# Retention and a hard-swish MLP on one core: the first pieces' Q loads issued later, two copies moved to VectorE, the last stores spread over three queues

## The chip, the cores and the metric

The kernel runs on one core of a Trainium2 chip. A core has TensorE (matmuls, PE in the profile, its weight loads PEld), VectorE (DVE), ScalarE (ACT), GpSimd (POOL) and SyncE (SP), each working through its own instructions in order, and 16 DMA engines that all queues share. The metric is the device time of one execution in microseconds (us), the median of repeated runs.

## The reference, cut to what matters

Inputs are q, k, v of shape (8, 8, 576, 64): batch, heads, sequence, head size. Weights are w_in (512 x 2048) and w_out (2048 x 512). All are float32.

```python
scores = (1/8) * q @ k.T                    # per batch and head, 576 x 576
gamma = 1 - 2 ** (-5 - head)
ret = scores * (gamma ** (i - j) if i >= j else 0)
x = (ret @ v)                               # heads side by side: 4608 tokens x 512
h = x @ w_in
g = h * clip(h + 3, 0, 6) / 6
out = g @ w_out                             # 4608 x 512
```

## The kernel before

The sequence of each batch is cut into pieces of 128 positions (four per batch), plus one of 64 that is paired with another batch's. Retention runs piece by piece: scores within the piece, masked; outputs from the masked scores and V; and a state that carries K and V of the earlier pieces on to the next. The decay is split into a factor on Q, a factor on V and a constant per piece on the state. Outputs are written as float16, transposed, into `xt`; every 512 tokens of `xt` go through the first GEMM with w_in (`g1`, line 577), the activation on ScalarE and VectorE (lines 585, 586), and the second GEMM with w_out (`g2`, line 635, or in seven products instead of eight, `g2_seven`, line 720). The retention of later pieces is woven in between the GEMMs. The order of instructions on each engine is the order in which the program writes them.

The change lies at both ends.

*The head.* Pieces 0 to 3 (`EARLY = 4`) come before the first GEMM and are built without transposing DMAs. `load_kv(c)` loads K and V by GpSimd's queue (line 103; the transfer converts them to float16). `load_q(c)` loads Q as float32 by SP's queue (line 120) into `qf`; with a second argument the load waits until that instruction has ended. `cast_q` makes it float16 on ScalarE (line 128). `q_by_pe` multiplies Q by a diagonal matrix `dq` on TensorE, which transposes and scales it (line 265), and copies the result to `qk[:, 0]` on ScalarE (line 272; for piece 3 in two halves, line 270). `k_by_pe` transposes K on TensorE (line 256) and copies it to `qk[:, 1]` on ScalarE (line 257). `scale_v` applies V's factor on VectorE (line 245). `scores` multiplies K by Q (line 343) and masks on VectorE (line 347), `inter` and `intra` make a piece's output from the state and the masked scores (lines 361, 372) and copy it to `xt` (line 377). `state_early` updates the state (lines 314, 318) and multiplies it by `gfull` on VectorE (line 323). Piece 3 has its own `scores_last` (line 283, masks in two halves on VectorE, line 286) and `out_last` (lines 297, 303, copies to `xt` line 306), after which the first GEMM starts. `fill_gfull` writes the decay constants of the state into `gfull`. `warm(n, cols)` runs n matmuls on zeros. GpSimd issues, in this order, K and V of pieces 0 to 3, then w_in in five parts (line 131), then w_out and the pieces from 4 on.

`newest[0]` holds the TensorE instruction that a later load is told to wait for. Before the change, Q 0 and Q 1 are loaded at once, Q 2 after the matmuls of `q_by_pe(0)` and Q 3 after the transposes of `k_by_pe(0)`.

*The tail.* In the last call of `g2_seven` each quarter of the output goes out by `store_quarter`: half of its rows by SP's queue and half by ScalarE's (line 688). The last product of the seven leaves two halves `xo` and `xtu` in PSUM; `copy_half(u)` copies each to SBUF on ScalarE (line 751), and `store` sends it out by SP's and ScalarE's queues (line 625).

Of the kernel before, what the change touches and what calls it, by code (L numbers as in the profile page):

```python
# [13 lines left out]
ALU = mybir.AluOpType  # L14
# [3 lines left out]
def kernel(  # L18
# [16 lines left out]
    nc = tc.nc  # L35
# [89 lines left out]
                reason="the first pieces have the queues")  # L125

    def cast_q(c):
        nc.scalar.copy(loaded[c]["q16"], plain_q[c])

    def load_win(f0, f1):  # L130
        return nc.gpsimd.dma_start(
# [11 lines left out]
    nc.gpsimd.iota(wide, pattern=[[1, P + 1]], base=-1, channel_multiplier=-1,  # L143
                   allow_small_or_imprecise_dtypes=True)
    load_q(0)
    load_q(1)
    load_kv(0)
    zeros = const.tile([P, MBLK], FP16)
    nc.vector.memset(zeros, 0.0)
# [6 lines left out]
    for h in range(H):  # L156
# [15 lines left out]
    nc.vector.tensor_tensor(out=ident16, in0=mask01, in1=mask_wide[:, 0:P], op=ALU.subtract)  # L172

    dq = const.tile([P, H, P], FP16)
    nc.vector.tensor_tensor(out=dq, in0=ident16[:, None, :].to_broadcast([P, H, P]),
                            in1=gq[:, :, None].to_broadcast([P, H, P]), op=ALU.mult)
    gqv = const.tile([P, 2, H, D], FP16)
    cast_q(0)
    nc.scalar.copy(gqv[:, 1], gv[:, :, None].to_broadcast([P, H, D]))
# [10 lines left out]
    nc.vector.memset(gfull, 0.0)  # L190

    def fill_gfull():
        nc.scalar.copy(gfull[0:HALF, :, 0:D],
                       gc[0:HALF, 0, :, None].to_broadcast([HALF, NPAIR, D]))
        nc.scalar.copy(gfull[HALF:P, :, D:2 * D],
                       gc[HALF:P, 0, :, None].to_broadcast([HALF, NPAIR, D]))

    def fill_gq():
        nc.scalar.copy(gqv[:, 0], gq[:, :, None].to_broadcast([P, H, D]))
# [52 lines left out]
    def k_by_pe(c, tag=None):  # L252
        kn = loaded[c]["kn"]
        pk = bank_or(tag, [P, NPAIR, P], FP16, name=f"trk_{c}")
        for p in range(NPAIR):
            newest[0] = nc.tensor.transpose(pk[:, p, :], kn[:, 2 * p:2 * p + 2, :], ident16)
        nc.scalar.copy(qk_of(c)[:, 1], pk)

    def q_by_pe(c):
        q16, qk = loaded[c]["q16"], qk_of(c)  # L260
        pq = bank([P, NPAIR, P], FP32, name=f"trq_{c}")
        for p in range(NPAIR):
            for h2 in range(2):
                r = slice(h2 * HALF, h2 * HALF + HALF)
                newest[0] = nc.tensor.matmul(
                    pq[r, p, :], q16[:, 2 * p + h2, :], dq[:, 2 * p + h2, :],
                    start=(p == 0), stop=(p == NPAIR - 1), skip_group_check=True)
        if c == EARLY - 1:
            for p in (0, 2):
                nc.scalar.copy(qk[:, 0, p:p + 2], pq[:, p:p + 2])  # L270
        else:
            nc.scalar.copy(qk[:, 0], pq)

    def scores_last(c):

# [60 lines left out]
    def scores(c, late=9):  # L336
        run_later(late)
        qk = st[c]["qk"]
        sc = psum.tile([P, 2, NPAIR, P], FP32, tag="sc", name=f"sc_{c}")
        for p in range(NPAIR):  # L340
            for h2 in range(2):
                r = slice(h2 * HALF, h2 * HALF + HALF)
                nc.tensor.matmul(sc[:, h2, p, :], qk[r, 1, p, :], qk[r, 0, p, :],
                                 start=True, stop=True)
        at = work.tile([P, 2, NPAIR, P], FP16, tag="at", bufs=3, name=f"at_{c}")
        st[c]["at"] = at
        later.append(lambda: nc.vector.tensor_tensor(
            out=at.rearrange("t a b s -> t (a b) s"), in0=sc.rearrange("t a b s -> t (a b) s"),
            in1=mask_b, op=ALU.mult))
# [328 lines left out]
    def store_quarter(kb, i, j, src):  # L678

        cols = slice(NH * j, NH * j + NH)  # L680
        if kb < B:
            r0 = kb * S + TH * i
            nc.sync.dma_start(out[r0:r0 + TH, cols].rearrange("(u p) n -> p u n", u=2), src)
        else:
            rest = out.rearrange("(m x s) n -> x s m n", x=2, s=S)
            for x in range(2):
                queue = nc.scalar if x else nc.sync
                queue.dma_start(rest[x, MAIN:S, 2 * i:2 * i + 2, cols],
                                src[x * HALF:x * HALF + HALF])

    def g2_seven(kb, last=False):

        gt = gts[kb]

        def w(i, j):
            return wout16[:, KH * i:KH * i + KH, NH * j:NH * j + NH]

        def a(i, j):
            return gt[:, KH * j:KH * j + KH, TH * i:TH * i + TH]

        def s(name):
            return sums[kb, name]

        acc = {}

        def get(name):
            if name not in acc:
                if last and name == "x":
                    acc[name] = [psum.tile([P, NH], FP32, tag=t, name=f"x{t}_{kb}")
                                 for t in ("o", "tu")]  # L710
                else:
                    whole = bank([P, 2, NH], FP32, name=f"{name}_{kb}")
                    acc[name] = [whole[:, 0], whole[:, 1]]
                    wholes[name] = whole
            return acc[name]

        def product(name, u, left, right, first):
            dst = get(name)[u]
            for c in range(KH):
                newest[0] = nc.tensor.matmul(  # L720
                    dst, left()[:, c, P * u:P * u + P], right[:, c, :],
                    start=(first and c == 0 and (u == 0 or name not in wholes)),
                    stop=(c == KH - 1), skip_group_check=True)

        kept, wholes = {}, {}

        def parts(name, tile):
            if name in wholes:
                return [(wholes[name], tile)]
            return [(acc[name][u], tile[:, u]) for u in range(2)]  # L730

        def keep(name):
            kept[name] = work.tile([P, 2, NH], FP32, tag="keep_" + {"m5": "m1"}.get(name, name), bufs=1,
                                   name=f"keep_{name}_{kb}")
            for src, dst in parts({"m5": "z"}.get(name, "x"), kept[name]):
                nc.scalar.copy(dst, src)

        def total(i, j, name, src):
            osb = work.tile([P, 2, NH], FP32, tag="osb", bufs=4, name=f"osb_{kb}_{i}_{j}")
            for (a0, dst), (_, a1) in zip(parts(src, osb), parts(src, kept[name])):  # L740
                nc.vector.tensor_tensor(out=dst, in0=a0, in1=a1, op=ALU.add)
            store_quarter(kb, i, j, osb)

        def copy_total():
            osb = work.tile([P, 2, NH], FP32, tag="osb", bufs=4, name=f"osb_{kb}_1_0")
            nc.scalar.copy(osb, wholes["x"])
            store_quarter(kb, 1, 0, osb)

        def copy_half(u):
            osb = work.tile([P, NH], FP32, tag="osb", bufs=4, name=f"osh_{kb}_{u}")  # L750
            nc.scalar.copy(osb, acc["x"][u])
            store(kb, 2 + u, slice(0, NH), osb)

        def unit(name, u, left, right, first, then=()):
            def do():
                product(name, u, left, right, first)
                for f in then:
                    f()
            return do

        plan = [
            ("x", lambda: a(0, 0), w(0, 0), True, [lambda: keep("m1")]),
            ("y", lambda: a(0, 1), w(1, 0), True,
             [lambda: total(0, 0, "m1", "y"), lambda: token_sums(kb, "s3")]),
            ("x", lambda: s("s2"), wts["t2"], False, [lambda: keep("u2")]),
            ("z", lambda: s("s1"), wts["t1"], True,
             [lambda: keep("m5"), lambda: token_sums(kb, "s4")]),
            ("x", lambda: s("s3"), wts["t3"], False, [lambda: total(1, 1, "m5", "x")]),
            ("z", lambda: s("s4"), w(1, 1), False, [lambda: total(0, 1, "u2", "z")]),
            ("x", lambda: a(1, 1), wts["t4"], False, [] if last else [copy_total]),  # L770
        ]
        units = []
        for n, (name, left, right, first, then) in enumerate(plan):
            for u in range(2):
                after = then if u else []
                if last and n == len(plan) - 1:
                    after = [lambda u=u: copy_half(u)]
                units.append(unit(name, u, left, right, first, after))
        return units
# [10 lines left out]
    for i in range(4):  # L790
        if i == 2:
            load(4)
        load_wout(4 * i, 4 * i + 4)

    scale_v(0)
    q_by_pe(0)
    load_q(2, newest[0])
    warm(2, MBLK)
    cast_q(1)
    k_by_pe(0)  # L800
    load_q(3, newest[0])
    fill_gfull()
    for c in range(EARLY):
        if c:
            inter(c - 1)
            intra(c - 1)
        if c < EARLY - 1:
            scores(c)
            run_later(9)
            if c:  # L810
                k_by_pe(c + 1)
            state_early(c)
            run_later(9)
            if not c:
                k_by_pe(c + 1)
            q_by_pe(c + 1)
            if c + 2 < EARLY:
                cast_q(c + 2)
            scale_v(c + 1)
        else:  # L820
            scores_last(c)
# [280 lines left out]
```

## Time and profile before

| what | value |
|---|---|
| median of 3 runs | 294.07 us (294.04 to 294.34) |
| the profiled execution's own time | 294.43 us |
| span of its instructions | 292.6 us |
| TensorE busy | 281.1 us, 96% |
| VectorE, ScalarE, GpSimd busy | 227.6, 169.1, 104.3 us |
| granted TensorE clock | 1.0 |
| start of the first GEMM (L577) | 18.17 us |
| first and second copy of the last halves (L751) | 287.45 and 288.49 us |

The profile's times run from the start of the span, so the execution's own time is 1.8 us more. Times of steps below come from this one execution; the median of the runs is 0.36 us under it.

### The profile page before, as it was taken

Reading aid. Unit: us, or ns where it says so; the run is one execution under the profiler, and the core shown is the slowest. Engines: PE = TensorE matmul, PEld = TensorE weight load, DVE = VectorE, ACT = ScalarE, POOL = GpSimd, SP = SyncE. Lnnn points to the kernel's source line nnn. Section 1 sums busy time; section 2 is a strip of 40 time slices with the busy share of each in tenths; the row PEclk is TensorE's granted clock in tenths of the full one; section 3 lists DMA queues with packets and bytes.
Section 4 is the critical chain, followed back from the end, with each engine's and each line's share of the span. In section 5 each row is a group of like instructions: output and inputs, shape, how many; then the busy total and the mean of one; then the engine's idle time right before and its main releaser. Section 6 shows DMA issues by size and latency. Waiting matters only on the chain.

```text
span 292.6 us, 8351 instructions
## 1 busy us (share of the span) xinstructions
PE 281.1 (96%) x3492; PEld 174.7 (60%) x3492; DVE 227.6 (78%) x377; ACT 169.1 (58%) x301; POOL 104.3 (36%) x130
## 2 busy tenths in 40 slices
PE   7699999999989999999999999999999999999993
PEld 2454445544544587458745874587458745874682
DVE  4858656798758997899789988998899588728860
ACT  6668537784357744774486448644864286338711
POOL 8753578159523432443234324455550000000000
PEclk9999999999999999999999999999999999999999
DMA  9999999999999989997999799979992240120014
GB/s 137 177 205 203 191 157 215 165 126 137 132 215 166 160 85 120 168 141 81 121 163 143 77 127 170 136 82 123 160 139 47 74 110 0 38 81 30 0 39 109
DMA packets 156631, 36.21 MB, mean 124 GB/s; under 512 B 143792, under 2 KB 155568, under 8 KB 156592
## 3 DMA queue, kind: packets, MB, share of 16 engines
q0 software_dynamic: 113104, 17.83, 89.3%
q1 hardware_dynamic: 42896, 17.31, 30.5%
q8 instruction: 27, 0.44, 0.7%
q10 hardware_dynamic: 592, 0.52, 0.5%
q14 instruction: 12, 0.10, 0.1%
HBM read 36.70 MB, written 9.44 MB: 158 GB/s over the span
## 4 chain that ended last, share of the span: by engine, by line
PE 91%; DMA 4%; POOL 2%; DVE 1%; issue 1%; ACT 0%; ACTq 0%; POOLq 0%
PE ph L577 41%; PE x L720 14%; PE pout L635 9%; PE z L720 8%; PE y L720 5%; DMA kn<-in_k_dram 3%; PE o L483 3%; PE sc L450 2%; PE o L504 1%; PE u L535 1%; PE ph L600 1%; POOL kn L103 1%; DMA out_dram<-osb 1%; PE xtu L720 1%; PE xo L720 1%
## 5 line engine op out<-in xcount | busy, mean ns | idle before, releaser
L577 PE MATMUL ph<-xt,win 128*128 128x512 f16 x560 | 122.3, 379 | 0.0
L586 DVE SCALAR_TENSOR_TENSOR gt<-u,ph 128x512 f16<-128x512 f32 x144 | 95.7, 685 | 22.6 <-ACT u L585 21.4
L585 ACT ACTIVATE u<-ph,cb 128x512 f32<-128x512 f32 x144 | 98.4, 688 | 25.7 <-PE ph L577 25.1
L577 PEld LDWEIGHTS <-win 128*128 128x128 f16 x560 | 54.7, 98 | 64.4
L103 POOL DMA_DIRECT2D kn<-in_k_dram x40 | 34.0, 850 | 40.7 <-PE ph L577 15.4
L103 POOL DMA_DIRECT2D qv<-in_v_dram x40 | 33.8, 846 | 38.8 <-PE ph L577 16.2
L720 PEld LDWEIGHTS <-sum_s 128*128 128x128 f16 x448 | 42.7, 98 | 5.3
L103 POOL DMA_DIRECT2D qv<-in_q_dram x36 | 30.2, 839 | 28.7 <-PE z L720 10.4
L720 PEld LDWEIGHTS <-gt 128*128 128x128 f16 x336 | 32.1, 98 | 5.5
L635 PE MATMUL pout<-wout,gt 128*128 128x512 f16 x128 | 29.6, 379 | 0.1
L720 PE MATMUL x<-wsum_t,sum_s 128*128 128x256 f16 x192 | 22.9, 273 | 0.0
L556 ACT CAST tm<-th 128x256 f16<-128x256 f32 x24 | 9.7, 405 | 20.3 <-DVE th L551 20.1
L635 PEld LDWEIGHTS <-gt 128*128 128x128 f16 x128 | 11.9, 98 | 13.2 <-issue 0.4
L456 DVE TENSOR_TENSOR at<-sc,mask 128x1024 f16<-128x1024 f32 x14 | 17.0, 1217 | 1.9 <-PE sc L450 1.9
L676 DVE TENSOR_TENSOR sum_s<-gt 128x1024 f16<-128x1024 f16 (+1 forms) x21 | 18.1, 864 | 0.2
L332 DVE TENSOR_TENSOR qv<-qv,gqv 128x1024 f16<-128x1024 f16 x26 | 17.8, 684 | 0.0
L514 ACT CAST xt<-o 128x512 f16<-128x512 f32 x28 | 15.0, 585 | 4.6 <-PE o L504 4.6
L567 DVE TENSOR_TENSOR ta<-u,th 128x256 f32<-128x256 f32 x24 | 10.2, 424 | 6.3 <-ACT th L554 5.2
L720 PE MATMUL z<-wout,sum_s 128*128 128x256 f16 x112 | 14.5, 274 | 0.0
L720 PE MATMUL y<-wout,gt 128*128 128x256 f16 x112 | 14.3, 273 | 0.0
L720 PE MATMUL z<-wsum_t,sum_s 128*128 128x256 f16 x112 | 13.6, 273 | 0.0
L720 PE MATMUL x<-wout,gt 128*128 128x256 f16 x96 | 11.5, 272 | 0.0
(118 smaller groups left out, 255.3 us busy)
## 6 DMA issues: line engine op xcount, KB each, us to landing
out_dram<-osb SPq DMA_DIRECT2D x32, 256.0 KB, 3.2
kn<-in_k_dram POOLq DMA_DIRECT2D x32, 128.0 KB, 5.9
qv<-in_v_dram POOLq DMA_DIRECT2D x32, 128.0 KB, 6.0
qv<-in_q_dram POOLq DMA_DIRECT2D x28, 128.0 KB, 5.9
wout<-in_moe_w_out_dram POOLq DMA_DIRECT2D x4, 512.0 KB, 15.2
win<-in_moe_w_in_dram POOLq DMA_DIRECT2D x3, 512.0 KB, 12.3
qf<-in_q_dram SPq DMA_DIRECT2D x4, 256.0 KB, 4.6
win<-in_moe_w_in_dram POOLq DMA_DIRECT2D x2, 256.0 KB, 8.3
```

Source lines behind the costliest of these rows:

```text
L103: loaded[c]["dma"].append(nc.gpsimd.dma_start(dst[p0:p0 + n], src[b, :, s0:s0 + n, :].rearrange("h s d -> s h d")))
L332: scaled = nc.vector.tensor_tensor(out=qv, in0=qv, in1=gqv, op=ALU.mult)
L456: nc.vector.tensor_tensor(out=at.rearrange("t a j p s -> t (a j p) s"), in0=sc.rearrange("t a j p s -> t (a j p) s"), in1=mask64[:, None, ...
L514: nc.scalar.copy(xt_at(cs[0], 0, 2 * P).rearrange("e p (j x s) -> e p j x s", j=2, x=2) [:, :, :, half, :], o[half].rearrange("e j p s -> ...
L556: nc.scalar.copy(tm, ta)
L567: nc.vector.tensor_tensor(out=ta, in0=st[c]["u"][1], in1=st[c]["sum"], op=ALU.add)
L577: newest[0] = nc.tensor.matmul(ph, win16[:, dmc, P * fc:P * fc + P], xt_of(kb)[:, dmc, :], start=(dmc == 0), stop=(dmc == NCC - 1))
L585: nc.scalar.activation(u, ph, ACTF.Relu, bias=cb[:, 0:1], scale=1.0 / 6.0)
L586: nc.vector.scalar_tensor_tensor(out=gts[kb][:, fc, :], in0=u, scalar=1.0, in1=ph, op0=ALU.min, op1=ALU.mult)
L635: nc.tensor.matmul(pout, gt[:, fc, P * mc:P * mc + P], wout16[:, fc, :], start=(fc == 0), stop=(fc == NFC - 1))
L676: nc.vector.tensor_tensor(out=s(which)[:, c0:c1], in0=x(), in1=y(), op=op)
L720: newest[0] = nc.tensor.matmul(dst, left()[:, c, P * u:P * u + P], right[:, c, :], start=(first and c == 0 and (u == 0 or name not in whol ...
```

## The change

Loads: Q 1 is no longer loaded at once but after `dq` has been computed on VectorE. Q 2 is loaded after the scores matmuls of piece 0 and Q 3 after the transposes of K 1; for that, `newest[0]` is now set in `scores` and no longer in `q_by_pe`.

Order in the loop over the first pieces: the cast of Q c+1 stands after `state_early(c)`, and with it come K and Q of piece c+1, K first for pieces 1 and 2, Q first for piece 3. For piece 3, K instead of Q is copied to `qk` in two halves. One more matmul of 512 columns on zeros follows `k_by_pe(0)`.

`fill_gfull` is done by VectorE instead of ScalarE, ahead of `scale_v(0)`.

Tail: of the quarter (0, 1) the second half of the rows is stored by GpSimd's queue instead of ScalarE's, and the second of the last two halves is copied by VectorE instead of ScalarE.

```diff
     def cast_q(c):
-        nc.scalar.copy(loaded[c]["q16"], plain_q[c])
+        return nc.scalar.copy(loaded[c]["q16"], plain_q[c])
...
     load_q(0)
-    load_q(1)
     load_kv(0)
...
-    nc.vector.tensor_tensor(out=dq, in0=ident16[:, None, :].to_broadcast([P, H, P]),
-                            in1=gq[:, :, None].to_broadcast([P, H, P]), op=ALU.mult)
+    load_q(1, nc.vector.tensor_tensor(
+        out=dq, in0=ident16[:, None, :].to_broadcast([P, H, P]),
+        in1=gq[:, :, None].to_broadcast([P, H, P]), op=ALU.mult))
...
     def fill_gfull():
-        nc.scalar.copy(gfull[0:HALF, :, 0:D],
-                       gc[0:HALF, 0, :, None].to_broadcast([HALF, NPAIR, D]))
-        nc.scalar.copy(gfull[HALF:P, :, D:2 * D],
-                       gc[HALF:P, 0, :, None].to_broadcast([HALF, NPAIR, D]))
+        nc.vector.tensor_copy(gfull[0:HALF, :, 0:D],
+                              gc[0:HALF, 0, :, None].to_broadcast([HALF, NPAIR, D]))
+        nc.vector.tensor_copy(gfull[HALF:P, :, D:2 * D],
+                              gc[HALF:P, 0, :, None].to_broadcast([HALF, NPAIR, D]))
...
     def k_by_pe(c, tag=None):
...
-        nc.scalar.copy(qk_of(c)[:, 1], pk)
+        if c == EARLY - 1:
+            for p in (0, 2):
+                nc.scalar.copy(qk_of(c)[:, 1, p:p + 2], pk[:, p:p + 2])
+        else:
+            nc.scalar.copy(qk_of(c)[:, 1], pk)
...
     def q_by_pe(c):
...
-        if c == EARLY - 1:
-            for p in (0, 2):
-                nc.scalar.copy(qk[:, 0, p:p + 2], pq[:, p:p + 2])
-        else:
-            nc.scalar.copy(qk[:, 0], pq)
+        nc.scalar.copy(qk[:, 0], pq)
...
     def store_quarter(kb, i, j, src):
...
-                queue = nc.scalar if x else nc.sync
+                queue = (nc.gpsimd if j > i else nc.scalar) if x else nc.sync
...
         def copy_half(u):
             osb = work.tile([P, NH], FP32, tag="osb", bufs=4, name=f"osh_{kb}_{u}")
-            nc.scalar.copy(osb, acc["x"][u])
+            if u:
+                nc.vector.tensor_copy(osb, acc["x"][u])
+            else:
+                nc.scalar.copy(osb, acc["x"][u])
...
+    fill_gfull()
     scale_v(0)
     q_by_pe(0)
-    load_q(2, newest[0])
     warm(2, MBLK)
-    cast_q(1)
     k_by_pe(0)
-    load_q(3, newest[0])
-    fill_gfull()
+    warm(1, MBLK)
     for c in range(EARLY):
         if c:
             inter(c - 1)
             intra(c - 1)
         if c < EARLY - 1:
             scores(c)
+            if not c:
+                load_q(2, newest[0])
             run_later(9)
-            if c:
-                k_by_pe(c + 1)
             state_early(c)
             run_later(9)
+            cast_q(c + 1)
+            if c == EARLY - 2:
+                q_by_pe(c + 1)
+            k_by_pe(c + 1)
             if not c:
-                k_by_pe(c + 1)
-            q_by_pe(c + 1)
-            if c + 2 < EARLY:
-                cast_q(c + 2)
+                load_q(3, newest[0])
+            if c < EARLY - 2:
+                q_by_pe(c + 1)
             scale_v(c + 1)
```

More of the change, by code (lines that the diff above doesn't have):

```diff
@@ L264, in q_by_pe @@
                 r = slice(h2 * HALF, h2 * HALF + HALF)
-                newest[0] = nc.tensor.matmul(
-                    pq[r, p, :], q16[:, 2 * p + h2, :], dq[:, 2 * p + h2, :],
-                    start=(p == 0), stop=(p == NPAIR - 1), skip_group_check=True)
-        if c == EARLY - 1:
-            for p in (0, 2):
-                nc.scalar.copy(qk[:, 0, p:p + 2], pq[:, p:p + 2])
-        else:
-            nc.scalar.copy(qk[:, 0], pq)
+                nc.tensor.matmul(pq[r, p, :], q16[:, 2 * p + h2, :], dq[:, 2 * p + h2, :],
+                                 start=(p == 0), stop=(p == NPAIR - 1), skip_group_check=True)
+        nc.scalar.copy(qk[:, 0], pq)
     def scores_last(c):
@@ L342, in scores @@
                 r = slice(h2 * HALF, h2 * HALF + HALF)
-                nc.tensor.matmul(sc[:, h2, p, :], qk[r, 1, p, :], qk[r, 0, p, :],
-                                 start=True, stop=True)
+                newest[0] = nc.tensor.matmul(sc[:, h2, p, :], qk[r, 1, p, :], qk[r, 0, p, :],
+                                             start=True, stop=True)
         at = work.tile([P, 2, NPAIR, P], FP16, tag="at", bufs=3, name=f"at_{c}")
```

## The prediction

> **What bounds the kernel now.** I read the chain of waits first, in order of time, because it says where a microsecond can be won at all.
>
> ```profile
> 6.75 7.55 DMA kn<-in_k_dram
> 14.30 0.05 issue
> 14.34 0.40 PE trk L256 x4
> ...
> 16.20 0.37 PE sc L283 x8
> 16.59 1.30 DVE at L286 x2
> 17.89 0.04 issue
> 17.93 0.30 PE o L303 x4
> 18.23 13.92 PE ph L577 x64
> ...
> 284.25 0.44 DVE osb L741
> 284.69 0.02 issue
> 284.71 2.75 DMA out_dram<-osb
> 287.46 0.37 ACT osh L751
> 287.86 0.51 ACTq L625
> ```
>
> From 18.2 to 284.2 us the chain is TensorE almost throughout, and the change touches nothing there. What it can move is the head (when the first GEMM starts, now 18.17) and the tail (when the last store goes out). A shift of the head passes on whole: the first GEMM runs 64 matmuls without a gap, and win, wout and the later pieces land before their use. In the head the last thing waited for is K of piece 3, landed at 14.30; 3.9 us of serial work follow.
>
> The timeline shows the head's other waits and the tail's one (the bracket is idle time before the instruction and what ended it).
>
> ```profile
> 10.51 0.62 ACT L128 CAST qv<-qf 128x512 f16<-128x512 f32 x1 [1.05 <-DMA qf<-in_q_dram]
> 11.09 0.40 PE L256 MATMUL trk<-ident,kn 128*128 128x128 f16 x4 [1.17 <-DMA kn<-in_k_dram]
> 13.40 0.62 ACT L128 CAST qv<-qf 128x512 f16<-128x512 f32 x1 [0.50 <-DMA qf<-in_q_dram]
> 287.45 0.37 ACT L751 COPY osh<-xo 128x256 f32<-128x256 f32 x1 [4.30 <-DMA out_dram<-osb]
> ```
>
> So Q 2 and Q 3 are already used the moment they land. The head is a race between transfers, and the question is in which order they land after the change. The DMA view of narrow stretches gives each transfer's issue and its time to landing; these are Q 2 (issued 5.33), Q 3 (6.60) and K 3 (6.75), then the packets per queue between 8 and 9 us, then a K transfer issued at 101.35 on an empty queue.
>
> ```profile
> qf<-in_q_dram SPq DMA_DIRECT2D x1, 256.0 KB, 5.2
> ```
> ```profile
> qf<-in_q_dram SPq DMA_DIRECT2D x1, 256.0 KB, 6.8
> kn<-in_k_dram POOLq DMA_DIRECT2D x1, 128.0 KB, 7.5
> ```
> ```profile
> q1 hardware_dynamic: 660, 0.17, 102.2%
> q0 software_dynamic: 231, 0.03, 45.4%
> ```
> ```profile
> kn<-in_k_dram POOLq DMA_DIRECT2D x1, 128.0 KB, 3.7
> ```
>
> Issue plus landing gives the order of before: Q0 4.0, Q1 5.3, K0 6.1, V0 7.0, K1 7.9, V1 8.7, Q2 10.5, K2 11.0, V2 12.9, Q3 13.4, K3 14.3, V3 15.1. Neighbours of K and V land 0.9 apart. Q2 and K2 together take 11.0 - 8.7 = 2.3, so a Q among others costs 1.4. The DMA share is full from 2 us on: transfers go one after another, and Q 2 had the engines nearly to itself between 8 and 9 us (660 packets against 231).
>
> The rule that fits the order is first ready, first served. An unqueued GpSimd transfer has its first packets 1.6 after issue (101.35 to 102.93), an unqueued SP load 1.1 after (Q0: 0.74 to 1.88). By that V1 is ready at 5.8, Q2 at 6.4, K2 6.6, V2 7.5, Q3 7.7, K3 8.4, V3 9.2: Q2 landed between V1 and K2, Q3 between V2 and K3. At 42 to 45 us a store issued at 42.11 took 5.3 us against the page's median 3.2, behind GpSimd loads ready before it.
>
> **The head, part by part.** K0 is ready at 1.36 + 1.05 + 0.7 = 3.1, but its packets began at 3.7, behind Q1. With Q1 gone it starts as Q0 ends and lands near 5.2 (0.9 earlier). That gains nothing by itself: TensorE is in its warm-up matmuls until about 6.05, so transposes start there, not at 6.17, and the scores of piece 0 near 7.1, not 7.24.
>
> Q1 now waits for dq, which ends at 3.60; issued 3.63, ready 4.7, behind V0 (4.0), just ahead of K1 (4.9). Q2 waits for the scores of piece 0: issued near 7.55 instead of 5.33, ready 8.65. K2 (6.6), V2 (7.5) and K3 (8.4) are now all ahead of it. Q3 waits for the transposes of K1, which lands at 8.3: issued near 8.75 instead of 6.60, ready 9.85, behind V3 (9.2), ahead of win (issued 8.48, ready 10.0). Nothing else sits on SP's queue until 42 us, so its longer waits delay no one else. Landings by 0.9 and 1.35: K0 5.2, V0 6.1, Q1 7.4, K1 8.3, V1 9.2, K2 10.1, V2 11.0, K3 11.9, Q2 13.2, V3 14.1, Q3 15.5. K 3 comes 2.4 earlier, Q 3 2.1 later. Win keeps its place, since the same twelve transfers precede it.
>
> In the new order ScalarE casts Q 3 behind xt of piece 1, TensorE builds Q 3 ahead of K 3's transposes, and both wait for that cast. From the landing: cast 0.62, matmuls 0.41, copy of Q 0.59 less 0.1 overlap, the two K halves 0.27 + 0.38, the second four score matmuls 0.29, masks 0.61 + 0.68, last output matmuls 0.24, and seven handovers of 0.04: 15.5 + 4.3 = 19.8. The same addition on the rows of before comes out 0.15 late, so 19.6: **1.45 later than 18.17**. Within it the reorder does pay: from K 3's landing to the GEMM there were 3.9 us; with Q built first and K last, only about 3.2 of them would follow K 3. But K 3 is no longer last. Q 2 binds as much: cast from 13.2, its matmuls at 13.9, the output matmuls of piece 1 behind them until 15.0, their copy to xt (0.5 of ScalarE), and only then, at 15.5, the cast of Q 3.
>
> Hidden edits: the two gfull copies leave ScalarE (0.40 each at 7.08) where it then waited 0.50 for trk; on VectorE, at 0.42 at most each (the 128x256 f32 row), they fall into its 1.88 idle before 7.11. One more warm-up matmul (0.4) falls into TensorE's 0.68 before the scores. If those covers were gone they would cost 0.8 and 0.4.
>
> At one place the Trainium skill speaks otherwise. Its page "DMA: Bandwidth & Descriptors", section "Queues, rings and completion order", says that an engine goes round robin between the queues it has work for, packet by packet. The store at 42.11, alone on its queue, waited for whole GpSimd transfers, and Q 3 waited through V2; the trace does not agree. Under that rule Q 2 and Q 3 would not stand behind K3 and V3; what that gives is the time of rival (a).
>
> **The tail.** ScalarE was issuing the second half of the (0,1) quarter's store until 287.36 and so copied xo at 287.45, though its matmuls end at 286.84; xtu's copy came after both, 288.49 to 288.86. Now GpSimd issues that store, ScalarE copies xo at 286.88, and VectorE copies xtu at 287.75 (matmuls end 287.71), 0.42 by its 128x256 f32 row: 288.17, so 0.69 sooner. SP and ScalarE are free by then; nothing queues behind VectorE's wait. Landing 2.2 later gives 290.4 against 291.1. The GpSimd store is the unknown: issued 286.72, nearest row the last V load (64 partitions, 3.4 to landing), a bit more for 128 KB: 290.4 to 290.5. It may tie. I take **0.65 gained**; bounds 0.75 gained and, at K0's 4.8 to landing in a full queue, 0.4 lost.
>
> **Sum.** +1.45 - 0.65 = +0.8. The profiled execution took 294.43 (span 292.6 and 1.8 around it), 0.36 over the median of 294.07. It would become 295.2; the median 294.9.
>
> **Rivals.** (a) The SP queue gets its turn as soon as the transfer in service ends. Then Q2 lands 11.5, V2 12.4, Q3 13.7, K3 14.6. K3 is last, the shortened 3.2 us plus handovers follow, and the GEMM starts near 17.9, 0.25 sooner; with the tail -0.9, that is **293.2**, faster. For it: Q 2 once running pushed K2 aside. Against: the two waits above. It decides if Q 3's cast starts before 14.1.
> (b) Mixed: one of Q 2 and Q 3 gets ahead, so that Q 3 lands at 14.6. The GEMM starts at 18.7, +0.55, less 0.65: **294.0**, no change. For it: readiness is known to 0.2 us only, and engines differ by up to 1 us.
> (c) The GpSimd store lands last by over 0.7: the tail gives nothing, and with the forecast's head the time is **295.6**. It decides from a landing after 291.1; GpSimd's loads on empty queues, 3.4 and 3.7, speak against.
> Beside these, TensorE stood 0.94 us at 84.16 with no releaser, after an instruction fetch in a full DMA; such a stall can come or go with the phase, which widens either end a little.
>
> **Chances.** About 0.2% (0.6 us) is what a measurement of this kernel can tell from no change: slower begins at 294.66, faster ends at 293.48. Forecast 0.5, (a) 0.26, (b) 0.19, (c) 0.05. The forecast with Q 3 at 15.2 and the full tail gain gives 294.5, so a tenth of its chance is "same"; (a) with a smaller tail gain is "same" for a small part, and (b) leans to faster with a missing stall. Slower 0.5, same 0.21, faster 0.29. The range takes in (a) at the low end and the late GpSimd store at the high: 293.1 to 295.6; the forecast's own is 294.5 to 295.4.
>
> **What would show it.** Right: K 3's transposes no longer wait on a K transfer but run behind Q 3's matmuls near 16.4; the casts of Q 2 and Q 3 follow "DMA qf" near 13.2 and 15.5; L576 (the first GEMM) starts near 19.6; xtu's copy on VectorE ends near 288.2 plus the head's shift. Wrong: a cast of Q 3 before 14.1 (then a), or a first GEMM before 18.2; a last chain link that is GpSimd's store (then c).

## The result: 2.4% slower, and the profile after

The changed kernel takes 301.81 us (median of 6 runs, 301.11 to 303.87) against 294.2 us for the kernel before on the same chip (6 runs, 293.9 to 295.19): a ratio of 1.0244, 95% interval 1.021 to 1.0278. The forecast was 294.9 with a range that ended at 295.6. The sign is right, the size is not: 7.6 us lost where 0.8 were forecast.

The profiled execution took 301.36 us with a span of 299.6, 6.9 more than the 292.6 of before. The first GEMM (line 576 now) starts at 26.98 instead of 18.17, so the head loses 8.81. From there to the end of TensorE's last matmul the new kernel is 0.96 shorter, mostly because the stall behind an instruction fetch, 0.94 before, is now 0.22. From that end to the end of the span it is 0.91 shorter. 8.81 - 0.96 - 0.91 = 6.94, the whole difference.

First the chain of waits of the changed kernel, in order of time (start, length, what).

```profile
3.28 6.08 DMA kn<-in_k_dram
9.36 0.05 issue
9.40 0.62 PE trk L256 x4
10.04 11.49 DMA qf<-in_q_dram
21.56 0.63 ACT qv L128
22.18 0.04 issue
22.23 0.64 PE trq L269 x8
22.86 0.54 PE trk L256 x4
...
24.40 0.54 PE sc L282 x8
...
26.56 0.38 ACT xt L305
26.94 0.04 issue
26.98 13.97 PE ph L576 x64
```

Before, the head's last wait was a K transfer that ended at 14.30. Now K 1 (issued at 3.28) lands at 9.36, its transposes release the load of Q 3 at 10.04, and that load takes 11.49 us, against 6.8 before. Everything behind it is serial. The timeline of ScalarE shows the three casts that wait for Q 1, Q 2 and Q 3 (in brackets, the idle time before and what ended it).

```profile
8.66 0.62 ACT L128 CAST qv<-qf 128x512 f16<-128x512 f32 x1 [1.98 <-DMA qf<-in_q_dram]
14.20 0.62 ACT L128 CAST qv<-qf 128x512 f16<-128x512 f32 x1 [2.50 <-DMA qf<-in_q_dram]
21.56 0.62 ACT L128 CAST qv<-qf 128x512 f16<-128x512 f32 x1 [4.31 <-DMA qf<-in_q_dram]
```

Before, these waits were none, 1.05 and 0.50. What the transfers did shows in the DMA view: per queue the packets, the MB and the time that the packets took. The first pair is the changed kernel from 16 to 17 us, the second from 18 to 19; q1 carries nothing but Q 3 here, and q0 (GpSimd's) w_in.

```profile
q0 software_dynamic: 216, 0.13, 89.2%
q1 hardware_dynamic: 215, 0.06, 40.8%
```
```profile
q0 software_dynamic: 161, 0.15, 89.7%
q1 hardware_dynamic: 163, 0.04, 31.3%
```

In these two stretches the queues take turns, one packet each. But w_in's packets carry 512 or 1024 B and Q 3's 256 B, so Q 3 gets 0.04 to 0.06 MB of the 0.19 that move in a microsecond, and its 256 KB take nearly 6 us, from 14 to 19.8 us for the most part. Fifteen of the sixteen engines were done with it at 20.43, the last at 21.53.

Next, three rows of a table of stretches: the kernel before from 3 to 6 us, then the changed one from 3 to 6 and 9 to 12. The columns are the stretch, its length, busy time and instructions of TensorE (then its weight loads, VectorE, ScalarE, GpSimd), TensorE's granted clock, the DMA share and GB/s. The 1.00 from 3 to 6 us is hardly a measurement: the first clock records come at 6.1 and 5.6 us, and until then the matmuls on zeros start 0.43 us apart, against 0.22 at the full clock.

```profile
3.00:6.00 3.00, 2.70 (x14) 0.70 (x12) 1.77 (x11) 2.00 (x6) 3.00 (x5) 1.00 1.91 189
```
```profile
3.00:6.00 3.00, 3.00 (x19) 1.12 (x17) 2.52 (x13) 1.92 (x5) 3.00 (x5) 1.00 1.42 112
9.00:12.00 3.00, 2.35 (x32) 1.81 (x32) 1.82 (x4) 1.93 (x4) 2.95 (x5) 0.51 2.04 178
```

Two things are new. Without Q 1 the transfers move 112 GB/s from 3 to 6 us instead of 189: 3 us of 77 GB/s are 231 KB, nearly one Q. And TensorE's granted clock (the share of its full clock that it is allowed) is 0.5 from 9.0 to 26.1 us, over nearly the whole rest of the head; the slices of the page show it too.

```profile
PEclk9657999999999999999999999999999999999999
```

Last the tail, from the timeline of the changed kernel.

```profile
294.72 0.37 ACT L753 COPY osh<-xo 128x256 f32<-128x256 f32 x1 [3.73 <-PE xo L719]
294.85 0.62 POOL L687 DMA_DIRECT2D out_dram<-osb  x1 [69.11 <-DVE osb L740]
295.60 0.42 DVE L751 COPY osh<-xtu 128x256 f32<-128x256 f32 x1 [1.05 <-PE xtu L719]
```

ScalarE's copy of xo waits for its matmuls now and no longer for a store's issue, and VectorE's copy of xtu starts 0.04 after the matmuls end. GpSimd's store landed at 297.59 and the last store at 298.46, so it is not the last.

### The profile page after: what moved, and what is told of

Same layout as the page of the kernel before. It is cut to its first block, busy times and chain, and to the rows that moved or that the text cites. A ratio compares the mean times of both kernels' runs of the same rounds, so it can differ in the third digit from the quotient of the medians.

```text
span 299.6 us, 8352 instructions
## 1 busy us (share of the span) xinstructions
PE 285.0 (95%) x3493; PEld 177.5 (59%) x3493; DVE 228.6 (76%) x380; ACT 167.9 (56%) x298; POOL 104.7 (35%) x131
## 3 DMA queue, kind: packets, MB, share of 16 engines
q0 software_dynamic: 113152, 17.96, 86.0%
## 4 chain that ended last, share of the span: by engine, by line
PE 90%; DMA 6%; POOL 1%; issue 1%; DVE 1%; ACT 0%; POOLq 0%
PE ph L576 40%; PE x L719 14%; PE pout L634 9%; PE z L719 9%; PE y L719 4%; DMA qf<-in_q_dram 4%; PE o L482 2%; DMA kn<-in_k_dram 2%; PE sc L449 2%; PE o L503 1%; PE u L534 1%; PE ph L599 1%; PE xtu L719 1%; PE xo L719 1%; PE trk L256 1%
## 5 line engine op out<-in xcount | busy, mean ns | idle before, releaser
L103 POOL DMA_DIRECT2D kn<-in_k_dram x40 | 34.0, 850 | 48.3 <-PE ph L576 13.4
L687 POOL DMA_DIRECT2D out_dram<-osb x1 | 0.6, 617 | 69.1 <-DVE osb L740 69.1
L634 PEld LDWEIGHTS <-gt 128*128 128x128 f16 x128 | 11.9, 98 | 13.0
L675 DVE TENSOR_TENSOR sum_s<-gt 128x1024 f16<-128x1024 f16 (+1 forms) x21 | 18.2, 865 | 0.2
L346 DVE TENSOR_TENSOR at<-sc,mask_wide 128x1024 f16<-128x1024 f32 x7 | 8.6, 1222 | 9.2 <-PE sc L342 9.1
L566 DVE TENSOR_TENSOR ta<-u,th 128x256 f32<-128x256 f32 x24 | 10.2, 425 | 6.2 <-ACT th L553 5.2
```

The lines of the kernel that those rows point to most:

```text
L103: loaded[c]["dma"].append(nc.gpsimd.dma_start(dst[p0:p0 + n], src[b, :, s0:s0 + n, :].rearrange("h s d -> s h d")))
L566: nc.vector.tensor_tensor(out=ta, in0=st[c]["u"][1], in1=st[c]["sum"], op=ALU.add)
L634: nc.tensor.matmul(pout, gt[:, fc, P * mc:P * mc + P], wout16[:, fc, :], start=(fc == 0), stop=(fc == NFC - 1))
L675: nc.vector.tensor_tensor(out=s(which)[:, c0:c1], in0=x(), in1=y(), op=op)
```

## The experiments

The theory after the result: the loss is the landing of Q 3, which meets w_in in the queues because it is issued too late; the half clock is a smaller part; the other edits are harmless. The rivals: the half clock is the main loss; one late Q is harmless and only all three together cost; the tail or the hidden edits cost. Beside each ratio (this kernel over the kernel before on the same chip, with its 95% interval) the tables give profile times in us: issue and landing of Q 3, landing of K 3, start of the first GEMM ("GEMM"), and the stretch in which TensorE's clock was half (the time before it first rose to full is left out where it rose in the head). The ratio is of many executions, the times are of one. So "none" holds for that one execution: over 23 executions of the kernel before on one chip, the mean granted clock lay between 0.981 and 1.0.

| kernel | ratio | Q 3 issued | Q 3 landed | K 3 landed | GEMM | half clock |
|---|---|---|---|---|---|---|
| before | 1 | 6.60 | 13.4 | 14.30 | 18.17 | none |
| changed | 1.0244 | 10.04 | 21.53 | 14.36 | 26.98 | 9.0 to 26.1 |

### First four: undo one part each

**Q 3 issued right behind Q 2.** The changed kernel, with both loads behind the scores of piece 0.

```diff
             if not c:
                 load_q(2, newest[0])
+                load_q(3, newest[0])
...
-            if not c:
-                load_q(3, newest[0])
```

> The changed kernel with one load moved: Q 3 is issued right behind Q 2, after the scores of piece 0, instead of after the transposes of K 1. Theory T (Q 3, issued at 10.04, became ready behind w_in's transfers and shared the DMA engines with them until 21.5): issued near 7.5 it is ready before w_in (10.0), lands at 15.5 to 16.5, the first GEMM starts at 20 to 21.5 instead of 27.0, and the time falls by about 6 us, to 295 to 296. Rival R1 (the loss is TensorE's half clock between 9.0 and 26.1 us): the idle times that lower the clock remain, so the time falls by 1 to 2 us at most, to 299 to 300. Rival R2 (the loss is the new order, Q before K for piece 3 and the casts behind the state): hardly any change, 301.

**All three Q loads as before**, the rest of the change kept. Not shown below: `dq` no longer releases a load of Q 1, and `q_by_pe` sets `newest[0]` again.

```diff
     load_q(0)
+    load_q(1)
     load_kv(0)
...
     q_by_pe(0)
+    load_q(2, newest[0])
     warm(2, MBLK)
     k_by_pe(0)
+    load_q(3, newest[0])
     warm(1, MBLK)
...
-            if not c:
-                load_q(2, newest[0])
...
-            if not c:
-                load_q(3, newest[0])
```

> The changed kernel with the three Q loads issued as in the kernel before (Q 1 at once, Q 2 after the matmuls of Q 0, Q 3 after the transposes of K 0); order of casts and copies, decay constant by VectorE, extra warm-up matmul and tail stay changed. Theory T: all of the loss goes; Q 3 lands near 13.4, K 3 near 14.3 and is the last, the first GEMM starts at 17.5 to 18.0 against 18.17 before, and with the tail's 0.7 to 0.9 the time is 292.5 to 293.3, faster than the kernel before. R1: the clock stays low only if the idle times do; by T's landings it is back at full and this run does not separate the two. R2 (order is the loss): still slower than before, 297 or more.

**The two tail edits alone**, in the kernel before.

```diff
-                queue = nc.scalar if x else nc.sync
+                queue = (nc.gpsimd if j > i else nc.scalar) if x else nc.sync
...
-            nc.scalar.copy(osb, acc["x"][u])
+            if u:
+                nc.vector.tensor_copy(osb, acc["x"][u])
+            else:
+                nc.scalar.copy(osb, acc["x"][u])
```

> The kernel before with the tail's two edits alone (half of quarter (0,1) by GpSimd's queue, the second half copied by VectorE). The prediction's term: 0.65 us gained (0.75 at most, 0.4 lost if the GpSimd store lands late). The changed kernel's trace has 4.07 us from the last matmul to the end of the span against 4.94, so 0.87: 293.3 to 293.6. Rival: GpSimd's store sets the end, and nothing is gained: 294.1.

**w_in behind Q 3.** The changed kernel, with GpSimd's weight loads held until the transposes of K 1 have ended, which Q 3's load also waits for.

```diff
-    load_win(0, WQ // 2)
-    load_win(WQ // 2, WQ)
...
+    def load_weights(after):
+        first_win = load_win(0, WQ // 2)
+        tc.add_manual_dep(
+            first_win.ins, after.ins.name,
...
+        load_win(WQ // 2, WQ)
...
                 load_q(3, newest[0])
+                load_weights(newest[0])
```

> The changed kernel with GpSimd's first w_in load (and with it all later ones) held until the transposes of K 1 have ended, the instruction that Q 3 also waits for; Q 3 is issued as late as in the changed kernel, near 10. Theory T (sharing with w_in makes it land at 21.5): Q 3 now meets only K 3 and V 3 and lands at 15.5 to 16.5, the first GEMM starts at 20 to 21.5, unless the first w_in part, held 1.6 us, lands later than that (18.5 to 19 expected), time 295 to 296.5. If the late issue by itself were the cause: Q 3 still lands after 19 and the time stays over 299. R1: 299 to 301, since TensorE idles as long.

| kernel | ratio (95% interval) | Q 3 issued | Q 3 landed | K 3 landed | GEMM | half clock |
|---|---|---|---|---|---|---|
| Q 3 with Q 2 | 1.0083 (1.0051 to 1.0114) | 7.19 | 15.96 | 14.79 | 20.89 | 14.6 to 18.0 |
| Q loads as before | 0.9963 (0.9945 to 0.998) | 6.7 | 13.49 | 14.23 | 17.96 | none |
| tail alone | 0.9983 (0.9957 to 1.001) | 6.9 | 13.98 | 14.36 | 18.23 | none in the head |
| w_in behind Q 3 | 1.0111 (1.0077 to 1.0146) | 10.34 | 18.71 | 14.92 | 24.34 | 10.7 to 24.3 |

With the Q loads as before, what is left of the change makes the kernel 0.4% faster, with an interval below 1: the loss is wholly in the three late loads. The tail alone is 0.17% under before with an interval that reaches past 1, and its profile has the stretch from the last matmul's start to the end of the span 0.48 shorter (4.73 against 5.21): the mechanism shows, the gain is too small for this measurement. Moving Q 3's issue forward by 2.85 took two thirds of the loss away; moving w_in out of its way took about half. In that last kernel 13 engines had Q 3 by 16.15, but one only at 18.71, and the clock was half until the first GEMM. So both gained less time than the theory had forecast: w_in behind Q 3 lies between the theory and its rival that the late issue by itself is the cause. The row of Q 3 with Q 2 flatters it, since its profile is of the fastest of seven executions (295.3, median 297.15). In that profile the chain of waits no longer passes through Q 3 but through Q 2, which landed at 13.47.

### Next four: which lateness, and the clock

**Q 1 at once.** The changed kernel with the load of Q 1 unconditional again; Q 2 and Q 3 stay late.

```diff
     load_q(0)
+    load_q(1)
     load_kv(0)
...
-    load_q(1, nc.vector.tensor_tensor(
+    nc.vector.tensor_tensor(
```

> The changed kernel with Q 1 loaded at once as before; Q 2 (after the scores of piece 0) and Q 3 (after K 1's transposes) stay late. Theory, that Q 1 among K and V made K 1 late, so that Q 3 was issued at 10.04 and met w_in: K 1 now lands near 8 (9.36 with the change), Q 3 is issued near 8.5, ahead of w_in's first part, and lands near 15.5 to 16.5; the first GEMM starts at 19.6 to 21, and the time is 0.2 to 1% over before. Rival, that Q 1's lateness is harmless: K 1 still lands after 9, Q 3 is issued after 9.7 and lands after 20, and the time stays 2 to 2.5% over before.

**Matmuls in TensorE's waits.** The changed kernel with matmuls on zeros where TensorE only waits.

```diff
                 load_q(2, newest[0])
+                warm(5, MBLK)
...
             if c == EARLY - 2:
+                warm(20, MBLK)
                 q_by_pe(c + 1)
...
             if c < EARLY - 2:
+                if c:
+                    warm(6, MBLK)
                 q_by_pe(c + 1)
```

> The changed kernel with matmuls on zeros in TensorE's waits of the head (5 behind the scores of piece 0, 6 ahead of Q 2's matmuls, 20 ahead of Q 3's), so that the granted clock has less reason to fall to 0.5 at 9 us. Theory, that the transfers are the loss and the clock a minor part: Q 3 is still issued near 10 and lands at 20 to 21.5, the first GEMM starts 1 to 2 us sooner than 26.98, and the time is 1.7 to 2.2% over before. Rival, that the half clock is the main loss: the first GEMM starts before 22 and the time is within 0.7% of before.

**The kernel before, with only Q 3 late.**

```diff
     k_by_pe(0)
-    load_q(3, newest[0])
     fill_gfull()
...
             scores(c)
+            if c == 1:
+                load_q(3, newest[0])
             run_later(9)
```

Not shown: `scores` sets `newest[0]`, as in the changed kernel.

> The kernel before with one load moved: Q 3 waits for the scores of piece 1 and is so issued near 10, as in the changed kernel (10.04), but after the issue of w_in's first parts; Q 1 and Q 2 are as before. Theory, that Q 3's issue behind w_in's is by itself the loss: Q 3 lands at 18.5 to 21, the first GEMM starts at 23 to 25.5, and the time is 1.5 to 2.4% over before. Rival, that it needs Q 1 and Q 2 to be late as well, with the whole queue pushed back: Q 3 lands before 16.5, and the time is within 0.7% of before.

**Only Q 1 late.** The kernel with the Q loads as before, but Q 1 waits for dq.

```diff
     load_q(0)
-    load_q(1)
     load_kv(0)
...
-    nc.vector.tensor_tensor(
+    load_q(1, nc.vector.tensor_tensor(
```

> The changed kernel with Q 2 and Q 3 loaded as before and Q 1 alone late (it waits for the decay product dq). Compared with the kernel that has all three as before (0.9963 of before). Theory, that Q 1 late delays V 0 and K 1 but nothing that is waited for last, as Q 3 is issued by 7: the first GEMM starts within 0.6 of 17.96, and the time is 0.995 to 0.999 of before. Rival, that Q 1 among K and V costs by itself: the first GEMM starts after 19, and the time is over 1.002 of before. Rival on the other side, that Q 1 late is the good part of the change: the first GEMM starts before 17.4 and the time is below 0.994.

| kernel | ratio (95% interval) | Q 3 issued | Q 3 landed | K 3 landed | GEMM | half clock |
|---|---|---|---|---|---|---|
| Q 1 at once | 1.0124 (1.0093 to 1.0155) | 8.5 | 16.62 | 11.74 | 22.24 | 12.4 to 22.6 |
| matmuls in the waits | 1.0198 (1.0162 to 1.0233) | 10.1 | 21.46 | 14.63 | 25.71 | 11.8 to 15.2 |
| before, Q 3 late | 1.0271 (1.0231 to 1.0312) | 11.0 | 22.41 | 13.18 | 27.60 | until 27.5 |
| only Q 1 late | 1.0055 (1.0035 to 1.0075) | 6.4 | 14.96 | 16.15 | 21.51 | 9.5 to 19.7 |

The kernel before loses as much as the whole change when Q 3 alone is late, so a late Q 3 is enough for the main loss. All three forecasts (landing, GEMM, ratio) were exceeded. It was issued at 11.0 rather than the 10 that was expected: TensorE ran at the half clock throughout the head in this profile, whose first clock record is at 27.54 (four transposes took 0.60 to 0.63, against 0.40 at the full clock). So the half clock has a part in this loss too: from Q 3's landing to the GEMM there were 5.19 us. Its DMA view from 12 to 13 us, and then from 16 to 17, shows both halves of Q 3's wait.

```profile
q0 software_dynamic: 949, 0.17, 210.7%
```
```profile
q0 software_dynamic: 161, 0.15, 91.7%
q1 hardware_dynamic: 161, 0.04, 30.9%
```

Issued at 11.0, Q 3 has not one packet between 12 and 13 (16 in all before 15): the transfers that GpSimd had queued go first. From 15 us on it has its turn, one packet for one of w_in's.

The matmuls on zeros kept the clock up over most of the head. Q 3 landed as late as with the change (21.46), and from its landing to the first GEMM there were 4.25 us instead of 5.45. So the half clock cost 1.2 us behind Q 3. The ratios differ by 0.0046, 1.35 us of 294, but their intervals overlap, so they agree with it without showing it. The rival that the clock is the main loss falls: all four executions had a granted clock of 0.994 or more and were 2% slower all the same.

Q 1 at once brought K 1's landing back to 8.07 and Q 3's issue to 8.54, just ahead of w_in's first issue at 8.55, and Q 3 landed at 16.62 instead of 21.53; the gain is half of the loss. The landing is at the edge of the forecast, the ratio above its 1%, and the GEMM came later than the expected 19.6 to 21, as the half clock held until 22.6: from Q 3's landing there were 5.62 us. And Q 1 late by itself is not harmless, which the theory had wrong: 0.9% over the kernel that differs in nothing else. Its row of the stretch from 3 to 6 us shows where it begins.

```profile
3.00:6.00 3.00, 2.92 (x16) 1.01 (x15) 2.52 (x13) 1.92 (x5) 3.00 (x5) 1.00 1.36 110
```

With 110 GB/s where the kernel with Q 1 at once has 191, every later transfer comes behind: K 1 at 9.78, K 3 at 16.15, V 3 at 17.02, where the kernel with all Q loads as before has 8.06, 14.23 and 15.07. Its chain of waits passes through K 2 (landed at 13.47, against 10.94), not through a Q. The clock fell as well (half from 9.5 to 19.7), and how the 0.9% divides between the landings and the clock is not shown.

### The other direction, both costs at once, and the size of packets

**All four Q loads at once at the start**, in the kernel with the Q loads as before.

```diff
     load_q(1)
     load_kv(0)
+    load_q(2)
+    load_q(3)
...
-    load_q(2, newest[0])
...
-    load_q(3, newest[0])
```

> The changed kernel with all four Q loads at once, at the start: the direction opposite to the change. Theory, that late Q loads lose because the transfers of the head are left unfed between 3 and 6 us (112 GB/s with the change, 189 in the kernel before) and then share engines with K, V and w_in: with Q early the DMA moves at least 185 GB/s from 3 to 6, Q 3 lands before 11, K 0 and V 0 come 1 to 2 us later, and K 3 is the last, at 14 to 14.6; the first GEMM starts at 17.4 to 18.4, and the time is 0.993 to 0.999 of before. Rival, that a K 0 delayed by four Q loads starves TensorE early and halves its clock, or pushes K 3 back: the first GEMM starts after 19, and the time is over 1.002 of before.

**Q 3 right behind Q 2, both early**, in the same kernel.

```diff
     load_q(2, newest[0])
+    load_q(3, newest[0])
     warm(2, MBLK)
     k_by_pe(0)
-    load_q(3, newest[0])
```

> The changed kernel with the Q loads as before, except that Q 3 is issued right behind Q 2 (near 5.9 instead of 6.7). Theory, that the last of Q 3 and K 3 sets the first GEMM, and that the total of the transfers is fixed: Q 3 lands 0.8 to 1.5 sooner than 13.49, K 3 stays within 0.3 of 14.23, and the first GEMM starts 0 to 0.4 sooner than 17.96; the time is 0.993 to 0.998 of before. Rival, that Q 3 pushes K 2 and K 3 back by as much as it gains: the first GEMM starts at 18.2 or later, and the time is 0.998 to 1.003 of before.

**w_in behind Q 3 and matmuls in the waits together**: the fourth and the sixth kernel's edits, with 10 matmuls instead of 20 ahead of Q 3's.

> The changed kernel with all its late Q loads, with both suspected costs taken away at once: w_in's loads are held until Q 3's issue, and matmuls on zeros fill TensorE's waits (5, 6 and 10 of them). Each alone left the time at 1.0111 and 1.0198 of before, where the change has 1.0244. Theory, that sharing with w_in and the half clock add up, and that what is left is the late issue itself: the ratio is near 1.0244 - 0.0133 - 0.0046 = 1.0065, between 1.004 and 1.009, with the first GEMM at 21.5 to 23.5. Rival, that they hide one behind the other: the ratio stays at 1.010 to 1.013. Rival, that they are the whole loss: it falls below 1.001.

**w_in in small packets.** The changed kernel, with the first half of w_in in eight loads of 128 columns.

```diff
-    load_win(0, WQ // 2)
-    load_win(WQ // 2, WQ)
-    for i in range(1, 4):
+    for i in range(8):
+        load_win(i * WQ // 4, (i + 1) * WQ // 4)
+    for i in range(2, 4):
         load_win(i * WQ, i * WQ + WQ)
```

> The changed kernel with the first half of w_in loaded in eight parts of 128 columns (256 B to a row of the tile, where the change has two parts with 512 B and one with 1024 B): the same bytes in the same order, Q 3 issued near 10 as in the change. Theory, that Q 3 takes turns with w_in packet by packet, so that w_in's larger packets take three quarters of the bytes: with packets of equal size Q 3 gets about half and lands at 17 to 19 instead of 21.5, the first GEMM starts at 22 to 24.5, and the ratio is 1.008 to 1.017. Rival, that Q 3 simply has to wait until the transfers ahead of it are through, whatever their packets: it lands at 20.5 or later, the first GEMM starts after 25.8, and the ratio stays at 1.020 or more.

| kernel | ratio (95% interval) | Q 3 issued | Q 3 landed | K 3 landed | GEMM | half clock |
|---|---|---|---|---|---|---|
| all Q at once | 1.0036 (1.0012 to 1.0061) | 2.9 | 10.34 | 14.86 | 21.53 | 9.8 to 16.6 |
| Q 3 behind Q 2 | 0.9956 (0.993 to 0.9982) | 5.8 | 12.64 | 14.24 | 17.91 | none |
| w_in behind Q 3, matmuls | 1.0108 (1.0072 to 1.0143) | 10.2 | 17.82 | 14.73 | 23.09 | 11.9 to 15.3 |
| w_in in small packets | 1.0105 (1.0048 to 1.0161) | 10.0 | 18.54 | 14.50 | 22.78 | 11.4 to 18.2 |

The last is the test of taking turns: the same bytes in the same order, in smaller packets of the other transfer, and Q 3 lands 3.0 sooner, the GEMM starts 4.2 sooner and 1.4 points of the 2.44 are gone. Of the 4.2, 1.2 are the way from Q 3's landing (4.24 against 5.45), since the clock was full again from 18.2 on. Its DMA view between 16 and 17 us, to set beside the changed kernel's:

```profile
q0 software_dynamic: 428, 0.11, 105.3%
q1 hardware_dynamic: 263, 0.07, 49.9%
```

Q 3 has 0.07 MB of 0.18 there, where it had 0.06 of 0.19, and 313 packets against 240 in the microsecond before. The turns are not one for one over the sixteen engines any more: the first of them was done with Q 3 at 15.71, four by 16.84. One thing stays apart from the packets' size: the loads themselves are smaller too, and the eight are issued from 8.48 to 15.96, where the change has the same half of w_in issued by 9.95. So less of w_in stood ahead of Q 3 at any time, and this run does not separate that from the packets.

Loading everything early is no cure. The transfers moved 194 GB/s from 3 to 6 us and Q 3 landed at 10.34, but K 0 came at 7.50 and K 1 at 11.24 instead of 6.18 and 8.06. The chain of waits passes through K 1, the clock fell, and the theory's forecast of a small gain was wrong; the rival had it right. Q 3 behind Q 2 gained 0.85 on Q 3, nothing on K 3, and 0.05 on the GEMM. V 2 (landed at 13.30) holds TensorE then: the timeline shows the state matmuls of piece 2, ahead of Q 3's at 14.35, waiting for the scaled V.

```profile
13.81 0.40 PE L315 MATMUL u<-qv,kn 128*128 128x128 f16 x4 [0.52 <-DVE qv L246]
14.04 0.38 PE L319 MATMUL u<-tbd,ident 128*128 128x512 f16 x1
14.35 0.41 PE L270 MATMUL trq<-dq,qv 128*64 128x128 f16 x8
```

The chain of the kernel with the Q loads as before passes through V 2 as well (landed at 13.32), so there too neither Q 3 nor K 3 sets the first GEMM. These two kernels are the fastest of all, and cannot be told apart.

The kernel with w_in behind Q 3 and matmuls in the waits did not add up: its ratio lies in the range of the rival that the two costs hide one behind the other. Its clock was full from 15.3 on and Q 3 landed at 17.82, but the matmuls on zeros ahead of Q 3's kept TensorE about 1 us too long (the cast ended at 18.46, Q 3's matmuls began at 19.54), and the measured 1.0108 is 1.3 us above the theory's 1.0065. So whether the two costs add stays open.

## Why the prediction was wrong, step by step

**The failed step** is "issued near 8.75 instead of 6.60, ready 9.85, behind V3 (9.2), ahead of win (issued 8.48, ready 10.0)". Q 3 was issued at 10.04, so by the prediction's own 1.1 it was ready at 11.1, behind w_in, whose first three parts were issued at 8.47, 9.21 and 9.95. Ahead or behind hung on 0.15 us, with a readiness that the text itself knew to 0.2 us, and it was never priced what follows if it goes the other way. That was the rival to write: "Q 3 behind w_in". From the sizes in the page of the profile it could have been bounded: w_in's first three loads are 1 MB, which at the 189 GB/s of 16 to 17 us take 5.5 us, an estimate.

The order in the queue is not all of it. With Q 1 at once, Q 3 was issued at 8.54, as early as forecast and ahead of w_in, and it landed at 16.62, not 15.5; the first GEMM still started at 22.24, and the kernel was 1.24% slower. So being behind w_in is worth 4.9 us of the landing (21.53 against 16.62), as far as Q 1's own return has no other part in it, and the rest lies in a landing 1.1 later than forecast and in 5.62 us from there instead of 4.1.

Its sizes. The first GEMM was forecast at 19.6 and came at 26.98, 7.38 late. Of these, 6.03 are Q 3's landing (21.53 against 15.5) and 1.35 the way from there (5.45 against 4.1), where the half clock, for which the prediction had no term, costs the 1.2 that the kernel with matmuls in the waits showed.

**K 1 at 8.3** was the first link of Q 3's issue to give: it landed at 9.36, and the transposes took 0.62 at the half clock instead of 0.40. The prediction let the transfers go one after another, Q 1 at 7.4, K 1 at 8.3, though in the kernel before both queues already moved packets side by side (302 of SP's queue and 675 of GpSimd's from 10 to 11 us). The landings after, as forecast and as measured:

| | K0 | V0 | Q1 | K1 | V1 | K2 | V2 | K3 | Q2 | V3 | Q3 |
|---|---|---|---|---|---|---|---|---|---|---|---|
| forecast | 5.2 | 6.1 | 7.4 | 8.3 | 9.2 | 10.1 | 11.0 | 11.9 | 13.2 | 14.1 | 15.5 |
| measured | 5.08 | 8.12 | 8.64 | 9.36 | 10.32 | 11.28 | 12.33 | 14.36 | 14.18 | 15.18 | 21.53 |

K 0 is right. From V 0 on all are 1 to 2.5 us late, and Q 3 is 6 us late. The prediction took Q 1's removal from the start as free: K 0 would take its place on the engines, and the others follow 0.9 apart. But the engines then moved 77 GB/s less for 3 us, and what is not moved there is moved later.

**"First ready, first served"** is half of the rule. A load that comes to a full queue does wait for what is queued ahead (no packet of Q 3 from 12 to 13 us in the kernel with Q 3 late). But once its packets start they take turns with those of GpSimd's next transfers, and then the packet size decides. The prediction set the Trainium skill aside here, its page "DMA: Bandwidth & Descriptors", section "Queues, rings and completion order", with its round robin packet by packet. The trace of the changed kernel (216 to 215, 161 to 163) agrees with the page, if the profile's packets are those that the page means. The prediction's "the trace does not agree" was drawn from two waits at the start of transfers, not from their course. It was also read as a rule in favour of the change (rival a), because only K and V were thought of as the neighbours: beside K's and V's 128 B packets a Q gets two thirds of the bytes (555 packets and 0.14 MB against 566 and 0.07 MB from 10 to 11 us, in the first experiment's kernel), beside w_in's a fifth to a third.

**Rivals.** (a) wanted Q 3's cast before 14.1, (b) Q 3 at 14.6: both out, with Q 3 at 21.53. (c), the GpSimd store landing last, is out with 297.59 against 298.46; its price comes to 295.5 by its own terms, not 295.6.

**The tail** is right, in the profile. The copy of xo is free of the store's issue. xtu's copy, forecast to end 0.46 after its matmuls, ended 0.46 after them (296.02 and 295.56); before it was 1.15. That is the 0.69 that was forecast, and 0.91 to the end of the span against the 0.65 that was taken. Alone, the gain is not clear of noise.

**The hidden edits** are free as said: the two copies on VectorE took 0.22 and 0.65 between 5.15 and 6.04, while V 0 was waited for until 8.15. The second is longer than the 0.42 that was its bound. The added matmul on zeros ended 0.46 us before TensorE's next work could start. K 3's transposes ran behind Q 3's matmuls, as forecast, only 6.5 us later.

**The stall** at the instruction fetch went from 0.94 to 0.22, which is luck: nothing in the change aims at it, and the range had allowed for it.

## What to carry to other kernels

A load that is delayed to make room for another must be followed to its new neighbours: give the issue times to a few tenths, list which transfers share the engines from there to the landing, and work the share out by packets, small against large. If its place ahead of a large transfer hangs on less than the error of your times, "behind it" is a rival with a price, and here the dearest one. Transfer time that goes unused early in a head that is bound by loads was not won back later in the kernels here, and a head that waits longer can lose TensorE's clock on top.

## What was not expected of the hardware

**A queue's turn is a packet.** With 256 B packets beside 512 B to 1 KB ones, a 256 KB load took 11.5 us from issue to landing, and 8.6 with the neighbour's first loads and packets cut smaller.

**TensorE's clock fell inside the head.** Wherever the clock fell inside the head, the trace has it at half for a multiple of 3.41 us (3.41, 6.83, 10.24, 13.65 or 17.07). The Trainium skill's page "TensorE: Matmul & The Clock Gate", section "Part 1: The HAM clock gate", has a free-running window of 3413 ns, and these lengths agree. It says that the clock falls after an idle window; here it fell after windows in which TensorE was busy for 0.95 to 1.9 us of the 3.41 (1.44 in the changed kernel, from 5.6 to 9.0), and it held after windows with 1.75 us or more in other kernels. So in the heads of these kernels the boundary lies near half a window of work. The windows do not lie alike: the first rise of the clock comes between 3.9 and 6.7 us in the profiles that show one, and close to the boundary this decides. In the profile of the kernel before, each full window of the head from 6.1 us on has 2.2 us of work or more.
